# Weights of a fused attention and gated-FFN kernel: staged loads and casts replaced by casting DMAs, with the first batches reordered around them

## The chip, the cores and the metric

The kernel runs on one core of a Trainium2 chip. The metric is the device time of one execution in microseconds (us). A difference between the two kernels is told from medians of repeated runs on the same chip.

## The reference, cut to what matters

Eight batches of twelve heads, each 448 positions by 64 elements, go through an attention without softmax: squared ReLU of the scores, divided by the sequence length. The result, as 3584 tokens of 768 elements, goes through an RMS norm, a gated feed-forward layer of width 1536 and an output projection.

```python
scores = scale * np.matmul(q, k.transpose(0, 1, 3, 2))      # scale = 1/8
attn = np.maximum(scores, 0.0) ** 2 / S                     # S = 448
x = np.matmul(attn, v)            # to (batch*position, head*element) = (3584, 768)
xn = x / np.sqrt(np.mean(x * x, -1) + 1e-06) * rms_g
g, val = xn @ w_gate, xn @ w_val                            # 768 x 1536 each
out = (g / (1 + np.exp(-g)) * val) @ w_out                  # 1536 x 768
```

All inputs and the output are float32 in DRAM. The kernel computes in bfloat16 with sums in float32.

## The kernel before, in words

Work goes batch by batch. Everything of a batch is kept transposed: 128 partitions hold the elements of a pair of heads, 448 columns hold the positions. There are six such pairs (`KT` = `HP` = 6), and twelve blocks of 128 hidden columns (`FT` = 12).

**Attention.** `pe_transposes` (L158) brings one head pair of q and k to PSUM by TensorE, and a copy (L165 on ScalarE for batch 1, L167 on VectorE for batch 0) puts it in `qkT`. Scores of a quarter of the positions (`scores` L201, `pair_scores` L221) go to a two-bank PSUM tile of a pool of two (`ps_s`); ScalarE, or VectorE for one quarter in four, applies the ReLU (L211, L231, L229) and VectorE squares it (L270). `attend` (L287) multiplies with v, and `leave` writes the scaled x (`xT`, L303) and its square (`x`, L304). A step that does one quarter of one head pair is called a visit here. From batch 2 on the transposes of q and k are made by DMA (L177, L181), with fills on the Pool queue (L189, L190).

**Swap.** Each gate and value matmul uses 64 of the 128 rows of TensorE, so two run side by side, one on each half of the partitions. Twelve heads are needed on both halves, so `swap` (L312) copies the upper half of `xT` to the lower half of `xD` and the reverse, by two DMAs.

**Gate and value.** `rounds` (L442) makes one block: six rounds on `xT` (own rounds), then six on `xD` (swapped rounds), two matmuls a round. Its weights are one 128-column slice of `wgv_sb`. `block_second` ends with SiLU on ScalarE (L483) and a product on VectorE (L485).

**Norm.** `norm_stat` sums the squares by TensorE (L405), takes the root on ScalarE (L412) and the reciprocal on VectorE (L416). `norm_apply` multiplies six tiles of `xT` in place (L421) and swaps them again, three pairs to a swap. For batch 0 the gate and value sums of blocks 0 to 2 are taken early, from x that is not yet normalized; `early_out` copies them out of PSUM (L454) and `early_rest` multiplies them with the reciprocal later (L460, L464, L466).

**Loads.** q, k, v and the first two 256-column slices of gate and value weights (blocks 0 to 3) come through casting DMAs on the Pool queue (L95, L111). The weights of blocks 4 to 11 come as float32 through the SP queue into four staging buffers (`fetch_raw`, L130), and Pool casts them (`cast_raw`, L141). `fetch_o` (L118) loads the output weights in six casting DMAs, between the casts. The staging buffers hold the space that the `kT` pool takes once they are closed (`unstage`), so the DMA transposes of batch 2 come after them.

**Order of the work.** Each engine runs its instructions in the order in which the program writes them. `weave` writes a main list and puts side steps between its units by position. For batch 0 the main list is `gate_value(0, EB)`, blocks 3 to 11, and the visits of batch 1 are its side steps. Then `out_tiles(0, 0, 3)` makes three output tiles (L405, L500), with the norm of batch 1 behind the first half tile; then follow the blocks of batch 1 with the visits of batch 2, and so on to batch 7. The loads of batch 2 (`fetch(2)`) stand behind the weights on the Pool queue, then the fills of batch 2, then `fetch(3)`.

Of the kernel before, what the change touches and what calls it, by code (L numbers as in the profile page):

```python
# [34 lines left out]
def kernel(  # L35
# [11 lines left out]
    nc = tc.nc  # L47
# [72 lines left out]
    stage = {}  # L120

    def fetch_raw(which, s):

        st = late["stage"].tile([P, H, P], FP32, name="wst", tag="wst")
        if which == "o":
            dst = st[:].rearrange("p a b -> p (a b)").rearrange("p (a b) -> p a b", a=2)
            i = nc.sync.dma_start(out=dst, in_=wo_rows(moe_w_out, s))
        else:
            for prt, src in gv_slices(s * P, (s + 1) * P):
                i = nc.sync.dma_start(out=st[prt], in_=src)  # L130
        stage[which, s] = st
        return i

    def cast_raw(which, s):
        src = stage.pop((which, s))[:]
        if which == "o":
            src = src.rearrange("p a b -> p (a b)").rearrange("p (a b) -> p a b", a=2)
            dst = wo_sb[:, 2 * s : 2 * s + 2, :]
        else:
            dst = wgv_sb[:, :, s * P : (s + 1) * P]  # L140
        return nc.gpsimd.tensor_copy(out=dst, in_=src)  # L141

# [6 lines left out]
    swapped = []  # L149
    HH = H // 2  # L150

    def pe_transposes(b, j):
# [155 lines left out]
    def swap(b, j0, j1, eng=None):  # L308

        swapped.append(b)  # L310
# [6 lines left out]
    def attention_first(b):  # L317
# [22 lines left out]
        add(leave, (HP - 2,))  # L340
        add(attend, (HP - 1,))
        add(leave, (HP - 1,))
        add(swap, 3, HP, nc.scalar)
        return units

    def attention_second(b):

        steps = [lambda: pe_transposes(b, 0)]
# [12 lines left out]
        for j in range(HP):  # L361
            for c in range(NCH):
                steps.append(lambda j=j, c=c: visit(j, c))
                if c == 0 and j + 1 < HP:
                    steps.append(lambda j=j: pe_transposes(b, j + 1))
# [41 lines left out]
    def norm_stat(b):  # L407
        psSS = ps_m.tile([P, S], FP32, name="psSS", tag="mm")
# [10 lines left out]
    def norm_apply(b, k0=0, k1=KT, eng=None):  # L419
        for kt in range(k0, k1):  # L420
            i = nc.vector.tensor_tensor(  # L421
                out=xTs[b][:, kt, :], in0=xTs[b][:, kt, :], in1=rstds[b][:], op=ALU.mult
            )
            if kt % 3 == 2:
                swap(b, kt - 2, kt + 1, eng)
        return i
# [7 lines left out]
    def rounds(b, fb, parts, r0, r1):  # L434

        for r in range(r0, r1):
            kt, own = r % KT, r < KT
            src = (xTs if own else xDs)[b]
# [18 lines left out]
    def early_rest(b, fb):  # L457

        t = early.pop(fb)
        nc.vector.tensor_tensor(  # L460
            out=t[:], in0=t[:], in1=rstds[b][:].unsqueeze(1).to_broadcast([P, 2, S]), op=ALU.mult
        )
        s = spool.tile([P, S], BF16, name="sil", tag="sil")
# [97 lines left out]
    def hold(i, until, reason):  # L561

        i, until = (x.ins if hasattr(x, "ins") else x for x in (i, until))
        tc.add_manual_dep(
            i,
            until.name,
            mybir.DependencyInfo(mybir.DependencyClass.Sync, mybir.DependencyReason.DATA),
            reason=reason,
        )

# [3 lines left out]
    for h0 in (0, HH):  # L574
        load("q", 1, h0, h0 + HH)
        load("k", 1, h0, h0 + HH)
    load("v", 1)
    def trans_fill(b, half):
# [3 lines left out]
    raws = [("gv", s) for s in range(4, FT)]  # L582
    NST, EB = 4, 3
    with tc.tile_pool(name="qkT", bufs=2, side="right") as tp, tc.tile_pool(
        name="early", bufs=EB, side="right"
    ) as ep:
        stages = ExitStack()
        late["stage"] = stages.enter_context(tc.tile_pool(name="stage", bufs=NST))
        late["qkT"], late["early"] = tp, ep
        warm(12)  # L590
        for n, fn in enumerate(attention_first(0)):
# [3 lines left out]
            if swapped and "raw" not in late:  # L595
                late["raw"] = [fetch_raw(*w) for w in raws[:NST]]
        fed = [0]
        held = {}
# [104 lines left out]
```

## Time and profile before

| what | value |
|---|---|
| median of 3 runs | 485.09 us (483.44 to 486.19) |
| the profiled execution: its own time | 487.38 us |
| the profiled execution: span from first to last instruction | 485.6 us |
| mean granted TensorE clock | 0.966 |
| DRAM read, written | 47.19 MB, 11.01 MB |
| busy: PE, DVE, ACT, POOL | 94%, 55%, 58%, 12% of the span |

All views below are of that one execution, with times from the start of its span. PE is TensorE, DVE VectorE, ACT ScalarE, POOL GpSimd, SPq and ACTq the DMA issuing of SP and ACT. A row of the timeline gives start, duration, engine, line, operation, what is written and read, and how many instructions were merged; in brackets stands the idle time ahead of it and what ended that. KB of a DMA and the GB/s of a stretch count bytes as they are written, so a casting load of 384 KB reads 768 KB. PEclk is the clock that TensorE was granted, as a share of full speed.

### The profile page before, as it was taken

The page shows a single profiled execution, that of the slowest core. Times are in us where ns is not written, and L with a number is a line of the kernel's source. Part 1 is how long each engine was busy: PE and PEld are TensorE (multiplying, and loading weights), DVE is VectorE, ACT ScalarE, POOL GpSimd, SP SyncE. Part 2 cuts the span into 40 slices and gives each one's busy share as a digit, 9 for nine tenths or more (in the row PEclk, how much of TensorE's full clock was granted, in tenths as well). Part 3 has the DMA queues.
Part 4 walks back from the last instruction along what each step waited for, and adds up shares of the span by engine and source line. Part 5 has one row for each costly group of instructions (what it writes and reads, how often), then busy time and mean ns, then how long its engine had stood idle before and what let it go on. Part 6 is the DMA issues. An engine that isn't in the chain of part 4 may idle for free.

```text
span 485.6 us, 10871 instructions
## 1 busy us (share of the span) xinstructions
PE 454.9 (94%) x4744; PEld 252.1 (52%) x4744; DVE 268.8 (55%) x309; ACT 282.0 (58%) x417; POOL 60.2 (12%) x79
## 2 busy tenths in 40 slices
PE   7986488995999999999999999999999999999996
PEld 2333245462555655565555655555556655565664
DVE  2865556651677546647675556647664667552210
ACT  3782557761676667756675667665775467562221
POOL 7301432303000030000300030002100000000000
PEclk8897779998899999999999999999999999999999
DMA  9999998999940199606990399508990640023013
GB/s 106 196 214 197 202 214 142 131 172 195 205 86 1 34 210 193 96 2 125 189 165 22 90 190 188 64 21 181 173 124 2 149 125 1 1 62 95 1 34 99
DMA packets 92431, 57.03 MB, mean 117 GB/s; under 512 B 36576, under 2 KB 85728, under 8 KB 92384
## 3 DMA queue, kind: packets, MB, share of 16 engines
q0 software_dynamic: 38672, 24.58, 35.3%
q1 hardware_dynamic: 53232, 30.73, 33.1%
q10 hardware_dynamic: 480, 1.03, 1.0%
q8 instruction: 37, 0.61, 0.5%
q14 instruction: 10, 0.08, 0.0%
HBM read 47.19 MB, written 11.01 MB: 120 GB/s over the span
## 4 chain that ended last, share of the span: by engine, by line
PE 78%; DMA 7%; ACT 4%; DVE 4%; SPq 3%; issue 1%; POOL 0%; ACTq 0%; POOLq 0%
PE psG L442 32%; PE psO L405 19%; PE psV L442 10%; PE psAV L287 7%; PE psS L242 6%; DMA xD<-xT 4%; SPq L130 3%; DMA wst<-in_moe_w_gate_dram 2%; DVE xT L421 1%; DVE rstd L416 1%; PE psSS L405 1%; PE psS L201 1%; DMA kb<-in_k_dram 1%; PE psW L559 1%; PE psS L221 1%
## 5 line engine op out<-in xcount | busy, mean ns | idle before, releaser
L442 PEld LDWEIGHTS <-wgv_sb 64*128 64x128 bf16 x2304 | 124.5, 95 | 114.6 <-issue 30.7
L442 PE MATMUL psG<-xD,wgv_sb 64*128 64x448 bf16 x558 | 123.8, 353 | 4.0 <-DMA xD<-xT 4.0
L442 PE MATMUL psV<-xD,wgv_sb 64*128 64x448 bf16 x558 | 123.3, 354 | 4.1 <-DMA xD<-xT 4.0
L442 PE MATMUL psV<-xT,wgv_sb 64*128 64x448 bf16 x558 | 122.9, 354 | 0.0
L442 PE MATMUL psG<-xT,wgv_sb 64*128 64x448 bf16 x558 | 122.9, 354 | 0.0
L485 DVE TENSOR_TENSOR hT<-sil,psV 128x448 bf16<-128x448 bf16 x93 | 57.6, 619 | 113.9 <-ACT sil L483 113.0
L405 PE MATMUL psO<-wo_sb,hT 128*64 128x512 bf16 (+1 forms) x1344 | 113.7, 326 | 0.0
L256 ACT ACTIVATE r<-psS 112x896 bf16<-112x896 f32 x108 | 96.1, 917 | 25.3 <-PE psS L242 25.2
L405 PEld LDWEIGHTS <-hT 128*64 128x64 bf16 x1344 | 74.8, 110 | 36.2 <-issue 4.1
L483 ACT ACTIVATE sil<-psG 128x448 bf16<-128x448 f32 x93 | 50.6, 544 | 67.6 <-PE psV L442 36.9
L260 DVE TENSOR_TENSOR r<-r 112x1792 bf16<-112x1792 bf16 x72 | 78.4, 1089 | 12.8 <-ACT r L256 11.7
L500 ACT COPY ost<-psO 128x512 f32<-128x512 f32 (+1 forms) x56 | 26.7, 477 | 50.3 <-PE psO L405 43.4
L242 PE MATMUL psS<-qT,kT 64*128 64x448 bf16 (+1 forms) x288 | 49.2, 354 | 2.0 <-DMA qT<-qT 1.7
L416 DVE RECIPROCAL rstd<-rstd 128x448 f32<-128x448 f32 x8 | 23.6, 2953 | 43.2 <-ACT rstd L412 43.2
L287 PE MATMUL psAV<-r,vb 112*64 112x448 bf16 x384 | 41.7, 356 | 1.3 <-DVE r L270 1.3
L303 ACT ACTIVATE xT<-psAV,ga_sb 128x448 bf16<-128x448 f32 x48 | 28.1, 630 | 25.0 <-PE psAV L287 25.0
L254 DVE TENSOR_SCALAR r<-psS 112x896 bf16<-112x896 f32 x36 | 39.0, 1084 | 5.3 <-PE psS L242 5.3
L189 POOL DMA_DIRECT2D qT<-qT x12 | 6.5, 539 | 267.4 <-DMA qT<-qb 117.3
L287 PEld LDWEIGHTS <-vb 112*64 112x64 bf16 x384 | 19.6, 110 | 21.9 <-issue 10.0
L421 DVE TENSOR_TENSOR xT<-xT,rstd 128x448 bf16<-128x448 bf16 x48 | 26.5, 618 | 3.4 <-DMA xD<-xT 3.1
L242 PEld LDWEIGHTS <-kT 64*128 64x128 bf16 (+1 forms) x288 | 17.7, 97 | 19.5 <-issue 8.5
L270 DVE TENSOR_TENSOR r<-r 112x1792 bf16<-112x1792 bf16 x23 | 26.8, 1182 | 0.6 <-ACT r L231 0.3
(51 smaller groups left out, 255.6 us busy)
## 6 DMA issues: line engine op xcount, KB each, us to landing
xD<-xT SPq DMA_DIRECT2D x30, 168.0 KB, 2.8
vb<-in_v_dram POOLq DMA_DIRECT2D x7, 672.0 KB, 18.2
qb<-in_q_dram POOLq DMA_DIRECT2D x6, 672.0 KB, 12.2
kb<-in_k_dram POOLq DMA_DIRECT2D x6, 672.0 KB, 13.9
qT<-qT POOLq DMA_DIRECT2D x24, 168.0 KB, 4.4
wst<-in_moe_w_gate_dram SPq DMA_DIRECT2D x8, 384.0 KB, 12.6
wst<-in_moe_w_val_dram SPq DMA_DIRECT2D x8, 384.0 KB, 13.6
out_dram<-ost SPq DMA_DIRECT2D x8, 336.0 KB, 4.6
```

The costliest lines, as they stand in the source:

```text
L242: nc.tensor.matmul(out=psS[: end - o, hf, :S], lhsT=flat[prt, o:end], rhs=qT[prt, 1 - hf : 3 - hf, h % HH], start=True, stop=True,)
L254: nc.vector.tensor_relu(out=r[:, cp], in_=src)
L256: nc.scalar.activation(out=r[:, cp], in_=src, func=ACT.Relu)
L260: nc.vector.tensor_tensor(out=r[:], in0=r[:], in1=r[:], op=ALU.mult)
L287: nc.tensor.matmul(out=part[hh * D : (hh + 1) * D, :], lhsT=ld["v", b][:, 2 * j + hh, c * D : (c + 1) * D], rhs=rsq[b, 2 * j + hh, c], sta ...
L303: nc.scalar.mul(out=xTs[b][:, j, :], in_=psAV[:, i, :], mul=ga_sb[:, j : j + 1])
L405: nc.tensor.matmul(out=ps[prt, :w], lhsT=lhsT[:, prt], rhs=rhs, start=start, stop=stop)
L416: nc.vector.reciprocal(out=rstd[:], in_=rstd[:])
L421: i = nc.vector.tensor_tensor(out=xTs[b][:, kt, :], in0=xTs[b][:, kt, :], in1=rstds[b][:], op=ALU.mult)
L442: nc.tensor.matmul(out=parts[part][:, :S], lhsT=wgv_sb[prt, h, fb * P : (fb + 1) * P], rhs=src[prt, kt, :], start=(r == 0), stop=(r == 2 * ...
L483: nc.scalar.activation(out=s[:], in_=psG, func=ACT.Silu)
L485: nc.vector.tensor_tensor(out=hT[:, fb, o : o + S], in0=s[:], in1=psV, op=ALU.mult)
```

## The change

Four things change, all of them before the output tiles of batch 0.

First, the staging goes away: no `fetch_raw`, no `cast_raw`, no staging pool. All weights come by casting DMAs on the Pool queue, gate and value in 256-column slices, queued at the start among the loads of batch 1. The `kT` pool is made at once.

Second, batch 0's swap of raw x is made pair by pair on SP, each behind its `leave`, instead of three pairs on SP and three on ACT. The two norm swaps move from ACT to SP.

Third, the normalized x of batch 0 goes to a second pair of buffers, so `norm_apply(0)` no longer waits for the readers of raw x. The early blocks now take all twelve rounds from raw x, block after block.

Fourth, the first two TensorE transposes of batch 1 move into the tail of batch 0's attention (their copies go to VectorE), and four visits and one more transpose of batch 1 go between the early blocks. The sum of squares of batch 0 moves to the other PSUM pool. `early_rest` is split, with its scaling ahead in the main list.

```diff
-        if b:
+        if b and j > 1:
             nc.scalar.copy(out=t[:], in_=psT[:])
...
             add(scores, j, (0, 1), (3,))
             if j > 1:
                 add(leave, (j - 2,))
-                if j == 4:
-                    add(swap, 0, 3)
+                add(swap, j - 2, j - 1)
...
         add(leave, (HP - 2,))
+        add(swap, HP - 2, HP - 1)
         add(attend, (HP - 1,))
         add(leave, (HP - 1,))
-        add(swap, 3, HP, nc.scalar)
+        add(swap, 5, HP)
...
+        src = xTs[b]
+        if b == 0:
+            xTs[b] = npool.tile([P, KT, S], BF16, name="xT", tag="xT", bufs=2)
+            xDs[b] = npool.tile([P, KT, S], BF16, name="xD", tag="xD", bufs=2)
+        for kt in range(KT):
+            nc.vector.tensor_tensor(
+                out=xTs[b][:, kt, :], in0=src[:, kt, :], in1=rstds[b][:], op=ALU.mult
             )
             if kt % 3 == 2:
-                swap(b, kt - 2, kt + 1, eng)
-        return i
+                swap(b, kt - 2, kt + 1)
...
         load("k", 1, h0, h0 + HH)
+    for s in range(2, 4):
+        fetch_gv(s)
     load("v", 1)
+    for s in range(4, NSL):
+        fetch_gv(s)
+    for s in range(FT // 2):
+        fetch_o(s)
+    late["kT"] = pool("kT", 2)
...
+            if n == len(first) - 3:
+                pe_transposes(1, 0)
+            if n == len(first) - 1:
+                pe_transposes(1, 1)
             fn()
...
-        rounds(0, 0, blocks[0], 0, KT)
+        raw_x = xTs[0], xDs[0]
+        blocks = [early_block(0)]
+        rounds(0, 0, blocks[0], 0, KT, raw_x)
         norm_stat(0)
...
-        rounds(0, 0, blocks[0], KT, KT + 3)
-        for fb in range(1, EB):
-            rounds(0, fb, blocks[fb], 0, KT + 3)
-        for fb in range(EB):
-            rounds(0, fb, blocks[fb], KT + 3, 2 * KT)
-            early_out(0, fb, blocks[fb])
-        feed(2)
-        norm_apply(0, 0, 3, nc.scalar)
+        steps.pop(0)()
+        rounds(0, 0, blocks[0], KT, 2 * KT, raw_x)
+        early_out(0, 0, blocks[0])
+        norm_apply(0)
+        for fb in range(1, EB):
+            blocks.append(early_block(fb))
+            steps.pop(0)()
+            rounds(0, fb, blocks[fb], 0, KT, raw_x)
+            steps.pop(0)()
+            rounds(0, fb, blocks[fb], KT, 2 * KT, raw_x)
+            early_out(0, fb, blocks[fb])
         main = gate_value(0, EB)
...
-        sides += [(9, unstage), (9.1, lambda: fetch(2))]
+        sides += [(9.1, lambda: fetch(2))]
```

On the Pool queue before, from the load of batch 1's v on. `wst` is a staging buffer, `wgv_sb` the gate and value weights, `wo_sb` the output weights.

```order
L95 DMA vb<-in_v_dram 112x12x256
L141 CAST wgv_sb<-wst 128x12x128 x3
L118 DMA wo_sb<-in_moe_w_out_dram 128x2x768
L141 CAST wgv_sb<-wst 128x12x128
L118 DMA wo_sb<-in_moe_w_out_dram 128x2x768
```

The same queue now, from four weight loads ahead of that v to batch 2's q:

```order
L111 DMA wgv_sb<-in_moe_w_gate_dram 64x12x256
L111 DMA wgv_sb<-in_moe_w_val_dram 64x12x256
L111 DMA wgv_sb<-in_moe_w_gate_dram 64x12x256
L111 DMA wgv_sb<-in_moe_w_val_dram 64x12x256
L95 DMA vb<-in_v_dram 112x12x256
L111 DMA wgv_sb<-in_moe_w_gate_dram 64x12x256
L111 DMA wgv_sb<-in_moe_w_val_dram 64x12x256
L111 DMA wgv_sb<-in_moe_w_gate_dram 64x12x256
L111 DMA wgv_sb<-in_moe_w_val_dram 64x12x256
L118 DMA wo_sb<-in_moe_w_out_dram 128x2x768 x6
L95 DMA qb<-in_q_dram 112x12x256
```

Nothing computes on Pool here any more, and batch 2's loads stand directly behind the last weights.

On ScalarE before, from batch 0's last `leave` (L304 writes the squares) to the first SiLU of an early block. `rstd` is the root of the norm, `gv` the early sums, `psS` scores.

```order
L304 ACTIVATE x_264<-psAV 128x448
L312 DMA xD<-xT 64x1344 x2
L412 ACTIVATE rstd<-psSS,eps_col 128x448
L415 ACT_TABLE_LOAD
L415 ACTIVATE warm_act<-eps_col 128x1
L454 COPY gv<-psE 128x448 x6
L312 DMA xD<-xT 64x1344 x2
L165 COPY qkT<-psT 128x896
L312 DMA xD<-xT 64x1344 x2
L464 ACTIVATE sil<-gv 128x448
L231 ACTIVATE r<-psS 112x896
```

The same stretch of ScalarE now (L280 is L304, L390 is L412, L207 is L231, L436 is L454, L468 is the SiLU of block 3):

```order
L280 ACTIVATE x_278<-psAV 128x448
L390 ACTIVATE rstd<-psSS,eps_col 128x448
L393 ACT_TABLE_LOAD
L393 ACTIVATE warm_act<-eps_col 128x1
L207 ACTIVATE r<-psS 112x896
L436 COPY gv<-psE 128x448 x2
L207 ACTIVATE r<-psS 112x896 x2
L436 COPY gv<-psE 128x448 x2
L141 COPY qkT<-psT 128x896
L436 COPY gv<-psE 128x448 x2
L207 ACTIVATE r<-psS 112x896 x2
L468 ACTIVATE sil<-psG 128x448
```

ScalarE issues no DMA there any more, and takes three ReLUs and one copy of batch 1 between the early sums.

On the SP queue now, from the load of the norm's gains to batch 2's first transposes:

```order
L530 DMA g_sb<-in_moe_rms_g_dram 128x6x1
L287 DMA xD<-xT 64x448 x12
L287 DMA xD<-xT 64x1344 x4
L153 DMA_TRANSPOSE qT<-qb 128x12x112
L157 DMA_TRANSPOSE kT<-kb 128x12x112
```

Before, sixteen staging loads stood between the first swap and the first transpose of this queue; now only swaps do.

More of the change, by code (lines that the diff above doesn't have):

```diff
@@ L148 @@
     raw, psAVs = {}, {}
-    swapped = []
     HH = H // 2
@@ L462, in early_rest @@
         )
+    def early_rest(b, fb):
+        t = early.pop(fb)
         s = spool.tile([P, S], BF16, name="sil", tag="sil")
@@ L594 @@
                 warm(2)
[L595 to L598, printed above, removed]
-        def feed(n):
-            while fed[0] < min(n, len(raws)):
-                i = cast_raw(*raws[fed[0]])
-                if fed[0] in held:
-                    hold(i, held[fed[0]], "casts on Pool keep out of the first batch's norm")
-                if fed[0] + NST < len(raws):
-                    fetch_raw(*raws[fed[0] + NST])
-                fed[0] += 1
@@ L609, in unstage, with early_block @@
-        def unstage():
-            feed(len(raws))
-            stages.close()
-            late["kT"] = pool("kT", 2)
-        steps = attention_second(1)
-        blocks = []
-        for fb in range(2):
-            psS = ps_s.tile([P, 2, 512], FP32, name="psE", tag="psS")
-            blocks.append((psS[:, 0, :], psS[:, 1, :]))
-        rounds(0, 0, blocks[0], 0, KT)
+        def early_block(fb):
+            return [ps_m.tile([P, S], FP32, name="psE", tag="mm")[:] for _ in range(2)]
+        raw_x = xTs[0], xDs[0]
```

73 lines of the change are left out of this document (18 added, 55 removed).

## The prediction

> **What bounds the kernel now.** I read the page's slices first, then the busy time by stretch, then the timeline where TensorE is not full.
>
> ```profile
> PE   7986488995999999999999999999999999999996
> ```
>
> Forty slices of 12 us: TensorE is full from the eleventh on. Only the first ten can give anything back.
>
> ```profile
> 12.00:24.00 12.00, 11.64 (x104) 4.32 (x105) 10.52 (x12) 8.96 (x13) 4.01 (x5) 0.83 1.45 195
> ...
> 36.00:48.00 12.00, 8.12 (x69) 3.76 (x69) 6.34 (x7) 3.08 (x5) 1.60 (x2) 0.81 1.22 197
> ...
> 60.00:72.00 12.00, 9.56 (x81) 4.57 (x81) 6.24 (x7) 5.72 (x8) 3.98 (x4) 0.70 1.19 216
> ...
> 108.00:120.00 12.00, 6.88 (x75) 4.16 (x72) 3.10 (x6) 2.25 (x4) 4.29 (x6) 0.93 1.13 183
> 120.00:132.00 12.00, 12.00 (x99) 6.09 (x96) 6.46 (x8) 6.91 (x9) 0.00 (x0) 0.78 1.33 241
> ...
> 144.00:156.00 12.00, 12.00 (x128) 6.35 (x127) 8.69 (x11) 8.17 (x12) 0.00 (x0) 1.00 0.01 1
> ```
>
> Columns: stretch, length, then busy time of PE, PEld, DVE, ACT and POOL, granted clock, DMA share, GB/s. A full stretch holds 128 matmuls. Two holes stand out, in 36 to 72 us and in 108 to 132 us, each with a lower clock and busy DMA engines. The timeline of TensorE and ScalarE names the waits of the first:
>
> ```profile
> 34.64 1.31 PE L442 MATMUL psE<-xT,wgv_sb 64*128 64x448 bf16 x12
> 35.88 1.33 PE L405 MATMUL psSS<-x,ones_bf 128*64 128x448 bf16 x12
> 37.14 0.74 PE L442 MATMUL psE<-xD,wgv_sb 64*128 64x448 bf16 x6
> ...
> 43.74 0.53 PE L442 MATMUL psE<-xD,wgv_sb 64*128 64x448 bf16 x1 [2.45 <-DMA xD<-xT]
> 45.70 3.51 PE L442 MATMUL psE<-xD,wgv_sb 64*128 64x448 bf16 x17 [1.44 <-DMA xD<-xT]
> ...
> 51.86 2.43 ACTq L312 DMA_DIRECT2D xD<-xT  x2
> ...
> 55.77 0.37 PE L221 MATMUL psS<-qkT 64*128 64x448 bf16 x2 [2.01 <-ACT r L231]
> ...
> 58.88 0.53 PE L442 MATMUL psV<-xD,wgv_sb 64*128 64x448 bf16 x1 [1.88 <-DMA xD<-xT]
> ...
> 62.92 0.53 PE L442 MATMUL psV<-xD,wgv_sb 64*128 64x448 bf16 x1 [1.19 <-DMA xD<-xT]
> ...
> 63.62 0.58 PE L442 MATMUL psV<-xD,wgv_sb 64*128 64x448 bf16 x1
> ```
>
> TensorE waits for the swap of raw x (43.74, 45.70), then for that of normalized x (58.88 to 62.92). ScalarE, stuck 2.43 us issuing swaps, holds up a ReLU in between. And after the waits a matmul takes 0.53 to 0.58 us.
>
> **The first hole, step by step.** Before, the last matmul of block 3 starts at 63.62 and runs into the next; I count the block to 64.0.
>
> Work between 34.64 and there: six own rounds take 35.88 - 34.64 = 1.24, the sum of squares 37.14 - 35.88 = 1.26. By the full stretch a matmul costs 12.00 / 128 = 0.094 us, so a block of 24 costs 2.25, four cost 9.0. A visit has two matmuls, 0.2 us. A transpose step, from the chain of waits:
>
> ```profile
> 17.86 0.52 PE psT L158 x16
> ```
>
> Before, this span holds four blocks, the sum, three visits and two transposes: 9.0 + 1.3 + 0.6 + 1.0 = 11.9 of 64.0 - 34.6 = 29.4 us. So 17.5 us are waits and slow clock.
>
> Now it holds six visits and one transpose (the other, first of batch 1, hides in the wait ahead of the last `attend`; the second adds 0.5 ahead of block 0). That is 0.5 + 9.0 + 1.3 + 1.2 + 0.5 = 12.5, so 47.1 if nothing waited. Two swaps can make it wait. Their prices, from the DMA issues (last column: us from issue to landing), the first pair's own issue ahead:
>
> ```profile
> 27.29 1.19 SPq L312 DMA_DIRECT2D xD<-xT  x2
> ...
> xD<-xT SPq DMA_DIRECT2D x2, 168.0 KB, 5.8
> ...
> xD<-xT ACTq DMA_DIRECT2D x2, 168.0 KB, 9.5
> ...
> xD<-xT SPq DMA_DIRECT2D x30, 168.0 KB, 2.8
> ```
>
> The first pair met mostly the Pool queue's casting loads; the second, on ACT some 8 us later, also the staging loads on SP; 2.8 is the median over the whole kernel. After the change only the Pool queue runs beside them, so I take 5.8, with 2.8 and 9.5 as bounds. The timeline gives the steps around them:
>
> ```profile
> 34.27 0.63 ACT L303 ACTIVATE xT<-psAV,ga_sb 128x448 bf16<-128x448 f32 x1
> ...
> 37.25 0.63 ACT L412 ACTIVATE rstd<-psSS,eps_col 128x448 f32<-128x448 f32 x1 [1.91 <-PE psSS L405]
> ...
> 37.91 2.95 DVE L416 RECIPROCAL rstd<-rstd 128x448 f32<-128x448 f32 x1 [4.16 <-ACT rstd L412]
> ...
> 40.96 1.70 DVE L421 TENSOR_TENSOR xT<-xT,rstd 128x448 bf16<-128x448 bf16 x3
> ...
> 45.73 1.69 DVE L421 TENSOR_TENSOR xT<-xT,rstd 128x448 bf16<-128x448 bf16 x3 [3.08 <-DMA xD<-xT]
> ```
>
> Raw x: the last pair is written at 34.9, its second DMA goes out 0.6 later (1.19 for two) and lands at 41.3. TensorE gets to the last round of block 0 at 34.6 + 0.5 + 1.2 + 1.3 + 0.2 + 1.0 = 38.8 and waits 2.5 us. Blocks 1 and 2 then end near 46.9, or 49 at a slow clock. Normalized x: the sum of squares ends at 37.6, root at 38.3, reciprocal at 41.2, six products at 44.6, with no wait between the two threes now (3.08 before, the second buffer's worth). The last swap DMA goes out at 45.2 and lands at 51.0; the last rounds take 0.6. Block 3 ends at 51.6, as this chain and not block 0's wait sets it. Gain 64.0 - 51.6 = 12.4, and three visits and a transpose (1.1) are done ahead: **13.5 us**. At 2.8 it would be 16.4, at 9.5 it is 9.8.
>
> Does the slow clock go too? Before, 0.70 over 60 to 72 is half speed for 7.2 of 12 us, so to about 67; from 64 on that costs 1.5 us. The row at 45.70 shows 17 matmuls in 3.5 us, twice the usual time, after waits of only 2.45 and 1.44. [...] The row speaks against it, so I give the 1.5 us against jams of VectorE in blocks 4 to 11, which gets three scalings there, and count nothing.
>
> **Removed at nothing.** Eight casts on Pool and the staging loads were off TensorE's path except through the contention priced above. Two copies of transposed q and k come to VectorE ahead of the reciprocal, which waits 4.16 us for the root; without that cover they would delay it by about 1.1 (two tiles, at the 0.57 of a product).
>
> **Do the weights come in time?** All now queue on Pool, in order. Until 24 us nothing moves but this queue, at 195 GB/s in 12 to 24 (190 KB a us). Sizes and landings from the DMA issues, one issue and the first output tile from the timeline:
>
> ```profile
> wgv_sb<-in_moe_w_gate_dram POOLq DMA_DIRECT2D x2, 384.0 KB, 13.8
> ...
> wo_sb<-in_moe_w_out_dram POOLq DMA_DIRECT2D x6, 384.0 KB, 9.1
> ...
> qb<-in_q_dram POOLq DMA_DIRECT2D x6, 672.0 KB, 12.2
> ...
> 9.20 0.81 POOL L111 DMA_DIRECT2D wgv_sb<-in_moe_w_gate_dram  x1
> ...
> 99.38 2.78 PE L405 MATMUL psO<-wo_sb,hT 128*64 128x512 bf16 x24
> ```
>
> By 24 us (9.20 + 13.8, and the next two loads) the first 3552 KB are in: 2016 of batch 0, 4 x 384 of weights. Then at 190 KB a us: batch 1's q and k (1344) at 31, blocks 4 to 7 (1536) at 39, v (672) at 43, blocks 8 to 11 at 51, output weights (2304) at 63, batch 2 (2016) at 73; 12 x 56 + 4 x 168 KB of swaps add up to 7. TensorE needs block 4 at 52, block 8 four blocks of 2.25 later at the earliest, 61, output weights at 99.4 less 13.5, 86. There is room of 10 us and more everywhere. Tightest is batch 1's first q and k, needed at about 32 by the transpose moved forward, 2 to 3 us ahead of block 0; their first halves stand before all added loads and are due at 24 + 672 / 190 = 28.
>
> **The second hole.** The norm of batch 1, in the timeline and (last two rows) the DMA issues:
>
> ```profile
> 86.73 0.95 POOL L95 DMA_DIRECT2D qb<-in_q_dram  x1
> ...
> 109.57 4.44 SPq L312 DMA_DIRECT2D xD<-xT  x4
> ...
> 110.81 0.97 POOL L95 DMA_DIRECT2D qb<-in_q_dram  x1
> ...
> 115.53 0.35 PE L242 MATMUL psS<-qT,kT 64*128 64x448 bf16 x1 [1.69 <-DMA qT<-qT]
> ...
> 118.33 0.48 PE L442 MATMUL psG<-xD,wgv_sb 64*128 64x448 bf16 x1 [2.46 <-DMA xD<-xT]
> 119.78 0.53 PE L442 MATMUL psV<-xD,wgv_sb 64*128 64x448 bf16 x1 [0.97 <-DMA xD<-xT]
> ...
> xD<-xT SPq DMA_DIRECT2D x4, 168.0 KB, 8.4
> ...
> qb<-in_q_dram POOLq DMA_DIRECT2D x1, 672.0 KB, 9.6
> ```
>
> Here 1.69 + 2.46 + 0.97 = 5.1 us are waits, and the clock of 0.78 over 12 us costs 2.6: 7.7 us. Batch 2's fills and batch 3's q collide with the swap. Batch 2's q was issued at 86.73, batch 3's 24.1 us later. Now batch 2's q lands near 72 (63, then its own 672 KB and most of the swaps; before 86.7 + 9.6 = 96.3); keeping the 14.5 us from there to batch 3's q, that one goes out at 86 to 88, and its three loads take 2016 / 190 = 10.6 us, to 97 or 99. The swap comes at 109.5 - 13.5 = 96. So the fills are out of the way (1.7) but the tail of `fetch(3)` may still meet the swap: 5.8 in place of 8.4 saves up to 2.6 more. I take **4.5 us**; bounds are 0 and 7.7. After 132 us TensorE is full and nothing changes.
>
> **Sum.** 13.5 + 4.5 = 18.0. Against the profiled execution, 487.4 - 18.0 = 469.4. That execution lies 2.3 above the median of the runs; taken off the median, 485.1 - 18.0 = **467**.
>
> **Rivals.**
>
> *The swaps still take 9.5 us* under a Pool queue that is full to 80 us. For: the DMA engines are no less busy than before. Against: the 5.8 row. First hole 9.8, second 4.5: 485 - 14.3 = 471.
>
> *The second hole stays*, moved up with the rest, because `fetch(3)` meets the swap again. 485 - 13.5 = 471.5. For: the 86 to 99 window against 96. Against: the fills are done earlier.
>
> *Both holes close*: quiet swaps and the clock kept: 16.4 + 7.7 + 1.5 = 25.6, so 459.5. For: staging moved twice the bytes of the cast weights. Against: the Pool queue stays full past the first norm.
>
> *Slower: the single Pool queue starves.* [...] It decides when the output weights come after 99.4 + 4.5 = 104 us, where the gain is spent: 7392 KB after 24 us, so below 7392 / 80 = 92 KB a us, half of what 12 to 24 shows. At 80 KB a us they come at 116, and the time is near 485 + 12 = 497. The 12 to 24 row excludes most of it: VectorE busy for 10.52 of 12 us, and the queue at 195 GB/s, with issues of 0.81 us. [...]
>
> **How the numbers follow.** Forecast (462 to 468.5) 0.52; slow swaps 0.13; second hole stays 0.13; both close 0.12; the change gives little (the moved transposes wait for q and k, and jams eat the rest) 0.04; slower 0.06. About 0.5% (2.4 us) is what a measurement of this kernel can tell from no change. Faster 0.90, same 0.04, slower 0.06. The range of 8 in 10 takes in the rivals on the faster side with 2.5 us of jams on top of 471.5: 458.5 to 475.
>
> **What would show it.** Right: block 3 ending near 52, no wait above 3 us in 36 to 60, first output tile near 86, waits at batch 1's norm under 3 us. Wrong: TensorE waiting for `wgv_sb` or `wo_sb` loads; swap landings of 9 us; the last tile of batch 0's blocks later than 92; ScalarE or VectorE the releaser of most waits in 52 to 86.

## The result, and the profile after

The changed kernel takes 471.8 us (median of 4 runs, 471.3 to 474.0), the kernel before 485.1 beside it: ratio 0.974, 95% interval 0.970 to 0.978. A second set of runs gave 471.3 and 0.973 (0.970 to 0.977). The change is 13.3 us faster, the forecast was 18.

The profiled execution of after took 472.2 us, its span is 470.2. Its row of TensorE in forty slices:

```profile
PE   6997899979999999999999999999999999999995
```

The slices below 9 in 36 to 72 us have thinned to one 7 and one 8; one hole is left, in the ninth slice. The same stretches as before show both places, after:

```profile
36.00:48.00 12.00, 9.19 (x71) 4.42 (x68) 7.31 (x9) 6.24 (x10) 3.10 (x5) 0.86 1.46 205
48.00:60.00 12.00, 10.64 (x127) 5.58 (x125) 8.05 (x9) 8.74 (x15) 4.00 (x5) 1.00 1.29 210
60.00:72.00 12.00, 11.01 (x131) 6.20 (x128) 9.64 (x14) 9.12 (x14) 0.93 (x1) 1.00 1.26 205
72.00:84.00 12.00, 11.24 (x116) 6.58 (x113) 7.30 (x10) 8.61 (x13) 1.09 (x2) 1.00 1.41 184
...
96.00:108.00 12.00, 8.79 (x79) 4.50 (x77) 2.71 (x5) 3.26 (x5) 0.00 (x0) 0.90 1.16 244
108.00:120.00 12.00, 11.65 (x115) 6.48 (x113) 9.68 (x11) 8.29 (x12) 0.00 (x0) 0.96 0.02 6
```

From 48 us on the clock is full (1.00) until the second hole. The DMA engines move 184 to 210 GB/s up to 84 us, in 44 to 60 us most of it for the queue of casting loads (2.60 of 3.31 MB), so the swaps of the first norm still run beside it. The timeline of TensorE through the first hole, up to the first output tile:

```profile
35.47 1.42 PE L424 MATMUL psE<-xT,wgv_sb 64*128 64x448 bf16 x12
...
40.60 0.35 PE L424 MATMUL psE<-xD,wgv_sb 64*128 64x448 bf16 x1 [1.41 <-DMA xD<-xT]
41.74 0.35 PE L424 MATMUL psE<-xD,wgv_sb 64*128 64x448 bf16 x1 [0.79 <-DMA xD<-xT]
42.36 0.35 PE L424 MATMUL psE<-xD,wgv_sb 64*128 64x448 bf16 x1 [0.27 <-DMA xD<-xT]
43.04 0.35 PE L424 MATMUL psE<-xD,wgv_sb 64*128 64x448 bf16 x1 [0.33 <-DMA xD<-xT]
...
45.01 2.71 PE L424 MATMUL psE<-xD,wgv_sb 64*128 64x448 bf16 x12
...
49.48 1.31 PE L424 MATMUL psE<-xD,wgv_sb 64*128 64x448 bf16 x12
...
53.91 0.35 PE L424 MATMUL psV<-xD,wgv_sb 64*128 64x448 bf16 x1 [0.70 <-DMA xD<-xT]
...
86.43 2.76 PE L380 MATMUL psO<-wo_sb,hT 128*64 128x512 bf16 x24
```

The waits for the swap of raw x add to 2.8 us, twelve matmuls then take 2.71 (1.31 one block later, at full speed), and block 3 waits 0.70 for the swap of normalized x. It ends near 54.5, before at 64.0. The first output tile starts at 86.43, before at 99.38.

The norm of batch 1 in the timeline of after, with the issues of its swap (SPq) and of batch 3's loads:

```profile
86.68 0.99 POOL L95 DMA_DIRECT2D qb<-in_q_dram  x1
91.24 0.96 POOL L95 DMA_DIRECT2D kb<-in_k_dram  x1 [3.58 <-issue]
92.19 0.94 POOL L95 DMA_DIRECT2D vb<-in_v_dram  x1
...
96.54 2.68 SPq L287 DMA_DIRECT2D xD<-xT  x4
...
103.15 0.35 PE L424 MATMUL psG<-xD,wgv_sb 64*128 64x448 bf16 x1 [2.29 <-DMA xD<-xT]
104.12 0.35 PE L424 MATMUL psV<-xD,wgv_sb 64*128 64x448 bf16 x1 [0.62 <-DMA xD<-xT]
105.49 0.51 PE L424 MATMUL psV<-xD,wgv_sb 64*128 64x448 bf16 x1 [0.23 <-DMA xD<-xT]
```

The DMA issues of after in 86 to 95 us, the loads of batch 3 (last column: us from issue to landing):

```profile
qb<-in_q_dram POOLq DMA_DIRECT2D x1, 672.0 KB, 9.2
kb<-in_k_dram POOLq DMA_DIRECT2D x1, 672.0 KB, 8.0
vb<-in_v_dram POOLq DMA_DIRECT2D x1, 672.0 KB, 16.0
```

The k and v of batch 3 land at 99.2 and 108.2 (issue plus landing), and the swap issued at 96.54 lies among them. Its landing stands in the DMA issues of 94 to 104 us:

```profile
xD<-xT SPq DMA_DIRECT2D x4, 168.0 KB, 6.8
```

Cutting each profiled execution in three makes all runs comparable: up to the first matmul on x (start), from there to the first output matmul (middle), and from there to the end of the span (rest). Before is 34.6 + 64.7 + 386.2, after is 35.5 + 51.0 + 383.8. So of the 15.4 us between the two spans 13.8 lie in the middle, 2.4 in the rest, and 0.8 is given back by a later start.

### The profile page after: what moved, and what is told of

Its sections match the earlier page's. It is cut to its first block, busy times and chain, and to the rows that moved or that the text cites. A ratio compares the mean times of both kernels' runs of the same rounds, so it can differ in the third digit from the quotient of the medians.

```text
span 470.2 us, 10856 instructions
## 1 busy us (share of the span) xinstructions
PE 450.9 (96%) x4748; PEld 252.0 (54%) x4748; DVE 265.8 (57%) x311; ACT 280.0 (60%) x415; POOL 53.6 (11%) x79
## 3 DMA queue, kind: packets, MB, share of 16 engines
HBM read 47.19 MB, written 11.01 MB: 124 GB/s over the span
## 4 chain that ended last, share of the span: by engine, by line
PE 83%; DVE 5%; DMA 5%; ACT 4%; issue 1%; POOL 1%; SPq 0%; POOLq 0%
PE psG L424 32%; PE psO L380 20%; PE psV L424 10%; PE psAV L263 9%; PE psS L218 6%; DMA xD<-xT 4%; DVE xT L404 2%; DVE rstd L394 2%; PE psSS L380 1%; PE psW L544 1%; PE psS L177 1%; DMA kb<-in_k_dram 1%; PE psT L134 1%; ACT r L207 1%; ACT r L187 1%
## 5 line engine op out<-in xcount | busy, mean ns | idle before, releaser
L424 PE MATMUL psG<-xD,wgv_sb 64*128 64x448 bf16 x558 | 121.9, 350 | 2.4 <-DMA xD<-xT 2.3
L424 PE MATMUL psV<-xD,wgv_sb 64*128 64x448 bf16 x558 | 121.6, 350 | 1.8 <-DMA xD<-xT 1.8
L424 PE MATMUL psV<-xT,wgv_sb 64*128 64x448 bf16 x558 | 121.6, 351 | 0.0
L468 ACT ACTIVATE sil<-psG 128x448 bf16<-128x448 f32 x93 | 50.7, 545 | 65.3 <-PE psV L424 36.9
L236 DVE TENSOR_TENSOR r<-r 112x1792 bf16<-112x1792 bf16 x72 | 78.4, 1090 | 12.7 <-ACT r L232 11.7
L485 ACT COPY ost<-psO 128x512 f32<-128x512 f32 (+1 forms) x56 | 26.8, 478 | 50.2 <-PE psO L380 44.0
L246 DVE TENSOR_TENSOR r<-r 112x1792 bf16<-112x1792 bf16 x23 | 24.5, 1086 | 0.1
## 6 DMA issues: line engine op xcount, KB each, us to landing
qb<-in_q_dram POOLq DMA_DIRECT2D x6, 672.0 KB, 12.4
```

What stands on the lines that cost most here:

```text
L236: nc.vector.tensor_tensor(out=r[:], in0=r[:], in1=r[:], op=ALU.mult)
L424: nc.tensor.matmul(out=parts[part][:, :S], lhsT=wgv_sb[prt, h, fb * P : (fb + 1) * P], rhs=src[prt, kt, :], start=(r == 0), stop=(r == 2 * ...
L468: nc.scalar.activation(out=s[:], in_=psG, func=ACT.Silu)
```

## The experiments

The three parts come from each kernel's profiled execution, the median from its runs. The kernels were timed in three groups of four, each group on one chip (the second and third on the same one) and beside the kernel before (484.6 us in the first, 485.9 in the second, 485.2 in the third), so ratios are given too.

| kernel | start | middle | rest | median | ratio to before, interval |
|---|---|---|---|---|---|
| before | 34.6 | 64.7 | 386.2 | 485.1 | |
| after | 35.5 | 51.0 | 383.8 | 471.8 | 0.974 (0.970 to 0.978) |
| after_again | 35.2 | 50.2 | 383.6 | 471.3 | 0.973 (0.970 to 0.977) |
| cast_only | 32.9 | 56.8 | 383.6 | 472.8 | 0.976 (0.972 to 0.981) |
| norm_in_place | 35.8 | 60.5 | 377.9 | 474.9 | 0.980 (0.976 to 0.984) |
| hold_fetch3 | 36.0 | 53.1 | 378.2 | 466.4 | 0.962 (0.958 to 0.966) |
| cast_hold | 35.1 | 55.1 | 377.9 | 470.5 | 0.968 (0.963 to 0.974) |
| batch2_first | 35.5 | 50.8 | 386.1 | 473.7 | 0.976 (0.972 to 0.979) |
| weights_wait | 36.7 | 50.4 | 384.2 | 471.6 | 0.972 (0.967 to 0.976) |
| visits_in_main | 34.2 | 55.3 | 382.2 | 471.9 | 0.973 (0.969 to 0.977) |
| hold_again | 36.9 | 50.4 | 377.8 | 465.8 | 0.959 (0.956 to 0.963) |
| cast_hold_again | 34.9 | 55.8 | 377.5 | 470.0 | 0.969 (0.966 to 0.972) |
| visits_hold | 36.8 | 55.6 | 377.6 | 471.0 | 0.970 (0.967 to 0.973) |
| before_hold | 35.2 | 63.5 | 378.3 | 479.0 | 0.985 (0.981 to 0.990) |

The start, 32.9 to 36.9, varies between executions of kernels that are alike up to there, and so does the middle: hold_fetch3 and hold_again are one kernel, with 53.1 and 50.4. A difference of under 3 us between two single values of that column proves nothing. The rest takes two kinds of values: 377.5 to 378.3 in the seven executions without a wait for the second norm's swap of over 0.5 us, 382.2 to 386.2 where the hole is there. So the hole costs 4 to 8.5 us, 6 of them in after and 8 in before.

Two theories stood at first. **Queue theory**: the gain is that the staged float32 loads no longer run beside the swaps, and what waits are left come from loads queued beside a swap. **Order theory**: the second buffer and the visits between the early blocks make the gain, and the leftover waits are set by the norm's chain of products.

**The change again**, for the spread of runs:

> The changed kernel itself, as the yardstick on this chip. Every theory: within 0.5% of 471.8 us; TensorE waits for the swap of raw x (about 2.8 us) and for that of normalized x (0.7 us) in the first hole, and 3.1 us for the swap of batch 1's norm.

471.3 us: the same.

**Only the loads** (cast_only). Before, with its staging taken out and the loads of the change put in; order, swaps and products in place as before:

```diff
     load("k", 1, h0, h0 + HH)
+for s in range(2, 4):
+    fetch_gv(s)
 load("v", 1)
+for s in range(4, NSL):
+    fetch_gv(s)
+for s in range(FT // 2):
+    fetch_o(s)
+late["kT"] = pool("kT", 2)
...
-        feed(2)
...
-        sides += [(9, unstage), (9.1, lambda: fetch(2))]
+        sides += [(9.1, lambda: fetch(2))]
```

> The kernel before with the weights loaded as the change does it, and nothing else of the change: old order, old swaps, norm in place. Queue theory (the gain comes mostly from taking the staged loads off the DMA engines): most of the gain, 474 to 478 us, swaps on ACT landing in 6 to 8 us instead of 9. Order theory (the gain comes from the second buffer and the visits between the early blocks; the loads only make room for it): 480 to 485 us, the wait of 3.1 us for the norm's second three products still there, and the second hole smaller by 2 to 3 us.

472.8 us, beyond what either theory gave: 1.5 from the changed kernel on the same chip, with intervals that overlap. Its timeline: the products on VectorE, then TensorE at the normalized swap and at the first output matmul:

```profile
39.19 3.30 DVE L421 TENSOR_TENSOR xT<-xT,rstd 128x448 bf16<-128x448 bf16 x6
...
49.93 0.35 PE L442 MATMUL psG<-xD,wgv_sb 64*128 64x448 bf16 x1 [2.55 <-DMA xD<-xT]
51.83 0.53 PE L442 MATMUL psV<-xD,wgv_sb 64*128 64x448 bf16 x1 [1.55 <-DMA xD<-xT]
53.66 0.53 PE L442 MATMUL psV<-xD,wgv_sb 64*128 64x448 bf16 x1 [0.33 <-DMA xD<-xT]
...
89.65 2.57 PE L405 MATMUL psO<-wo_sb,hT 128*64 128x512 bf16 x22
```

The wait of 3.08 us before the second three products, which the order theory expected to stay, is gone, though the products are still written in place: the last wait for the second half of raw x's swap ended 7.4 us after ScalarE began to issue it (33.16 to 40.55), before 10.8 (34.93 to 45.70). The normalized swap itself landed no faster (8.9 us, 8.1 and 9.2 before), but ScalarE issued it from 42.5 us on, from 49.3 before. Block 3 ends at 54.7, about as early as in after, but the first matmul on x of this execution also came 2.6 us earlier. Counted from the first matmul on x, block 3 ends after 29.4 us in before, 21.8 in cast_only (20.7 and 20.3 in the two later kernels with these loads and a hold) and 19.0 in after. So the loads alone give most of the gain up to there, without second buffer and without visits ahead. This run takes away the staging loads and the casts on Pool together, and batch 2 comes earlier with them; it doesn't tell these apart. Its main list is longer, 35.0 us from the end of block 3 to the first output matmul against 31.9 in after. The profiled execution was this kernel's longest (475.4).

**Products in place** (norm_in_place). After, with batch 0's products in `xT` and so behind the last reader of raw x:

```diff
     def norm_apply(b):
         src = xTs[b]
-        if b == 0:
-            xTs[b] = npool.tile([P, KT, S], BF16, name="xT", tag="xT", bufs=2)
-            xDs[b] = npool.tile([P, KT, S], BF16, name="xD", tag="xD", bufs=2)
...
         early_out(0, 0, blocks[0])
-        norm_apply(0)
         for fb in range(1, EB):
...
             early_out(0, fb, blocks[fb])
+        norm_apply(0)
```

> The changed kernel with batch 0's products written in place, so after the early blocks' last matmul on raw x instead of beside them. If the chain root, reciprocal, products, swap sets the end of block 3: the products start about 50 instead of 41.8 us, block 3 ends near 62 instead of 54.5, and the time is 5 to 8 us more (477 to 480). If TensorE has enough other work around block 3: under 2 us more (471 to 474).

474.9 us, 3.6 over after_again. In its timeline the wait for the swap is back, and the first output matmul comes ten us later:

```profile
58.80 0.53 PE L421 MATMUL psG<-xD,wgv_sb 64*128 64x448 bf16 x1 [4.87 <-DMA xD<-xT]
...
96.25 2.76 PE L380 MATMUL psO<-wo_sb,hT 128*64 128x512 bf16 x24
...
106.32 2.83 SPq L287 DMA_DIRECT2D xD<-xT  x4
```

The middle is 60.5, so in the new order the buffer is worth some 10 us there. But 5.7 come back in the rest: the second norm's swap is issued only at 106.32, after the last of batch 3's loads has landed (v, issued at 96.73, in 7.3 us); it lands in 2.8, and TensorE doesn't wait for it. Neither theory had seen that the two holes trade.

**Batch 3's loads behind the swap** (hold_fetch3). After, with a dependency:

```diff
-    fetch(3)
     weave(out_tiles(0, 0, full), [(1, lambda: norm_stat(1)), (1, lambda: norm_apply(1))])
+    hold(fetch(3)[0], applied[1], "third batch's loads keep out of the second norm's swap")
```

Here `applied[1]` is the last DMA of the swap, and the Pool queue sends batch 3's q only when that has landed.

> The changed kernel with batch 3's loads held back until the swap of batch 1's norm has landed. Queue theory: that swap lands in about 3 us instead of 6.8, the second hole's 4.9 us (3.1 of waits, 1.7 of slow clock) shrink to under 1, time 466 to 468 us. Rival, the hole is set by the norm chain and by TensorE running out of output tiles: the swap lands as late, time 471 to 473 us.

466.4 us, and no wait for the swap at the second norm: it landed in 2.6 us, where it took 6.7 in after_again. This and its repeat below are the fastest of all kernels here. That the second hole is batch 3's loads beside the swap is shown by taking away that one thing.

**Batch 2 ahead of the output weights** (batch2_first):

```diff
-    for s in range(FT // 2):
-        fetch_o(s)
...
+        fetch(2)
+        for s in range(FT // 2):
+            fetch_o(s)
...
-        sides += [(9.1, lambda: fetch(2))]
```

> The changed kernel with batch 2's three loads put ahead of the output weights on the Pool queue; nothing is held. In the changed kernel batch 2's q is issued at 56.9, lands at 74.0, and with it the transposes, the shifted copies and then batch 3's loads come late: those are issued from 86.7 on and land until 108, beside the second norm's swap (issued 96.5, landed 103). Queue theory: with batch 2 some 8 to 10 us earlier, batch 3's loads are issued near 77 to 80 and have landed before the second norm's swap is issued; the waits for xD of 3.1 us after 100 us and the half-speed matmuls behind them go, 467 to 469. The output weights then come later, near 72 to 76, still ahead of the first output tile at 86. Rival: batch 3's loads are set by the end of batch 0's and 1's use of their buffers and not by batch 2's landing; they stay at 86 to 92, the second hole stays, 471 to 472.5.

473.7 us: slower than either expected. Batch 2's q did land 12.5 us earlier (61.5 against 74.0), but its transposes then ran beside the output weights. The SP queue of this kernel:

```profile
61.59 3.43 SPq L153 DMA_TRANSPOSE qT<-qb  x1
65.29 12.13 SPq L157 DMA_TRANSPOSE kT<-kb  x1
77.48 7.68 SPq L153 DMA_TRANSPOSE qT<-qb  x1
85.21 6.58 SPq L157 DMA_TRANSPOSE kT<-kb  x1
```

In after these four begin at 74.0 and are all issued by 85.2. Here the last is issued by 91.8, so the fills behind them on the Pool queue go out at 96.5 and batch 3's three loads at 97.6 to 99.5, all at once on top of the swap issued at 96.4. TensorE waits longer than in after:

```profile
102.75 0.35 PE L424 MATMUL psV<-xD,wgv_sb 64*128 64x448 bf16 x1 [1.87 <-DMA xD<-xT]
107.05 0.53 PE L424 MATMUL psG<-xD,wgv_sb 64*128 64x448 bf16 x1 [3.58 <-DMA xD<-xT]
107.77 0.53 PE L424 MATMUL psV<-xD,wgv_sb 64*128 64x448 bf16 x1 [0.19 <-DMA xD<-xT]
```

More of batch 3 beside the swap, a longer wait: 5.6 us against 3.1, a rest of 386.1 against 383.8. The queue theory's cause stands; the date at which it thought the loads would come was wrong.

**Later weights behind the first swap** (weights_wait):

```diff
-    for s in range(4, NSL):
-        fetch_gv(s)
-    for s in range(FT // 2):
-        fetch_o(s)
...
+        for s in range(4, NSL):
+            fetch_gv(s, applied[0] if s == 4 else None)
+        for s in range(FT // 2):
+            fetch_o(s)
```

> The changed kernel with the weights of blocks 8 to 11, the output weights and so batch 2 behind them held on the Pool queue until the first norm's swap has landed. It measures what the loads that run beside that swap cost. Queue theory: the swap, which lands 7.8 us after its issue beside the casting loads, lands in 3 to 4 us; block 3 ends near 50.5 instead of 54.5 and the first output tile comes 3 us earlier, 468 to 469.5, if batch 2, some 5 us later than now, doesn't widen the second hole (issue of batch 3's loads at 91 to 96, all of them then beside the second swap; it costs back 0 to 3). [...]

471.6 us, no change. The swap did land early, by the DMA issues of 44 to 60 us:

```profile
xD<-xT SPq DMA_DIRECT2D x4, 168.0 KB, 2.6
```

In after it is 7.8 in the same place. Block 3 no longer waits at all, and yet its middle is that of after_again (50.4 and 50.2). The early blocks in its timeline tell why:

```profile
41.70 0.35 PE L429 MATMUL psE<-xD,wgv_sb 64*128 64x448 bf16 x1 [1.31 <-DMA xD<-xT]
...
44.05 2.79 PE L429 MATMUL psE<-xT,wgv_sb 64*128 64x448 bf16 x12
...
46.67 2.75 PE L429 MATMUL psE<-xD,wgv_sb 64*128 64x448 bf16 x12
```

The swap of raw x, issued before the hold does anything, still makes TensorE wait, and the half-speed matmuls behind that fill the time up to 49 (clock 0.77 over 36 to 48 us, 0.86 in after). In after the two chains, the norm's with its swap and TensorE's own through the early blocks, end within 0.7 us of each other (the wait at 53.91); by that, taking one away gains no more than 0.7. No run takes both away. Here the queue theory failed in the time: behind the held loads the swap did land early, in 2.6 us, and the time stayed as it was.

**The visits back in the main list** (visits_in_main). The early blocks without steps of batch 1 between them:

```diff
-        steps.pop(0)()
         rounds(0, 0, blocks[0], KT, 2 * KT, raw_x)
...
-            steps.pop(0)()
             rounds(0, fb, blocks[fb], 0, KT, raw_x)
-            steps.pop(0)()
```

The two lines in the loop run twice, so these are five steps, four visits and a transpose (the text on record counts one visit too few).

> The changed kernel with the four steps of batch 1 that it runs between the early blocks (three visits and a transpose) back in the main list; products in the second buffer and everything else as in the change. Theory that the visits cover the waits for the products and their swap: without them each early block comes earlier and waits longer for the swap, block 3 no earlier, and the main list has 4 steps (some 2.5 us) more to do, +1.5 to +2.5: 473 to 474.3. Rival, after the run cast_only: steps of batch 1 cost the same in either place, the early blocks come earlier by as much, and the matrix unit's order around the wait is worth nothing, within 0.8 of the changed kernel: 471 to 472.5.

471.9 us: by the median the rival was right, and the visits are worth nothing. By the parts they are worth 4.4 in the middle (55.3 against 51.0), with 1.6 back in the rest, where the hole is smaller, and 1.3 from an earlier start of that execution. This and norm_in_place led to a third theory, the **sink theory**: with the hole open, time gained ahead of it comes partly back as a longer wait in it, because batch 3's loads drain at their own date.

**Loads with the hold** (cast_hold): cast_only with the edit of hold_fetch3.

> This is the kernel of the run cast_only (before with all weights as casting loads and nothing else of the change: old order of the early blocks, products in place, old grouping of the swaps), with batch 3's loads held until the second norm's swap has landed. Loads theory: the reordering and the second buffer are worth the 1 us between cast_only (472.8) and the changed kernel (471.3 to 471.8) and no more; with the second hole closed in both, this kernel comes to 466.5 to 468.5, at most 2 above the run hold_fetch3 (466.4), with no wait for xD after 84 us. Order theory: the reordering pulls the first output tile forward by 3 us (89.65 in cast_only, 86.43 in the changed kernel) and the second hole hid that; with the hole closed the 3 us come out, and this kernel stays at 469 to 471.

470.5 us. It speaks for the order theory's number, but the runs of the two kernels met (467.2 to 471.4 against 465.0 to 469.3, on different chips), so the last four kernels ran together, with more rounds.

> The kernel of the run hold_fetch3 (466.4) a second time, beside the next three on one chip, since runs of one kernel differ by 1 to 2 us. Both theories: 465.5 to 468.

> The kernel of the run cast_hold (470.5: before with weights as casting loads and batch 3's loads held, nothing else of the change) beside hold_again. Sink theory, formed after eight runs: the second norm's swap cannot land before batch 3's loads have drained, near 103 to 107 us in every kernel whose first output tile starts between 86 and 90, so what the reordering and the second buffer gain before that is eaten by a longer wait there; with the hole closed it shows, and this kernel is 2.5 to 4.5 us over hold_again. Loads theory: the difference between the two earlier runs (4.1 us, 467.2 to 471.4 against 465.0 to 469.3) was chance; at most 1.5 us over hold_again.

> The changed kernel with the four steps of batch 1 moved out of the early blocks to the main list (the run visits_in_main: 471.9, no slower than the changed kernel, though its first output tile starts at 89.5 instead of 86.4) and with batch 3's loads held until the second norm's swap has landed. Sink theory: the 3 us that the visits are worth at the first output tile come out once the second hole is closed: 2 to 3.5 over hold_again, 468.5 to 470. Rival: the steps cost the same in either place and the later output tile is made up elsewhere: within 1 of hold_again.

> The kernel before with one edit: batch 3's loads held until the second norm's swap has landed. It tests the forecast's reading of the second hole, where before waits 1.69 us for a shifted copy and 2.46 and 0.97 for the swap (115 to 120 us) with half-speed matmuls behind them, 7.7 in all. Queue theory: those waits are the swap and the copies lying behind batch 3's q on the DMA engines (issued 110.8, the swap 109.6); they go, and the half-speed stretch with them, 478 to 480.5. Rival: the swap is late by itself, since its products are; 483.5 to 486.

hold_again 465.8, cast_hold_again 470.0, visits_hold 471.0, before_hold 479.0. In the first, the Pool queue waits for the swap, and the DMA issues of 94 to 104 us give the swap's landing:

```profile
103.10 0.97 POOL L94 DMA_DIRECT2D qb<-in_q_dram  x1 [17.23 <-DMA xD<-xT]
```

```profile
xD<-xT SPq DMA_DIRECT2D x4, 168.0 KB, 2.8
```

With the hole closed, the ratios of hold_again (0.959, 0.956 to 0.963) and cast_hold_again (0.969, 0.966 to 0.972) lie apart: the reordering and the second buffer are worth 4.2 us, as the sink theory said, where with the hole open 1.5 was left of them. By medians the hold itself takes 6.2 off before and 4.9 off after, but only some 2.5 off cast_only and 1 off visits_in_main (cast_only against a kernel on another chip, visits_in_main against one of another group), while the rest of each profile shortens by 4.6 to 7.9. The profiled executions of cast_only and visits_in_main, whose rest is compared there, were the longest of their kernels; how large the hole is in a typical run of these two stays open. The visits are worth 5.2, more than the 2 to 3.5 expected. The stretch of visits_hold and one wait in its timeline show what they cost in the main list:

```profile
60.00:72.00 12.00, 9.48 (x116) 5.09 (x117) 11.02 (x15) 8.91 (x13) 1.88 (x2) 1.00 1.26 205
```

```profile
66.51 0.36 PE L196 MATMUL psS<-qkT 64*128 64x448 bf16 x2 [1.94 <-DVE r L204]
...
92.39 2.78 PE L380 MATMUL psO<-wo_sb,hT 128*64 128x512 bf16 x24
```

TensorE is busy for 9.48 of 12 us there, 11.01 in after: it waits for the ReLUs and squares of batch 1 on VectorE and ScalarE. A visit in the main list costs its share of those; between the early blocks it lies in time that TensorE waits for swaps anyway. And before_hold bears out the forecast's reading of the second hole of before: one dependency takes 6.2 us off the median of the kernel before, and its profile has no wait for that swap above 0.48 us. But only four of its six runs show the gain, 476.6 to 479.1 us; the other two took 485.2 and 485.9, as long as before, at mean clocks of 0.973 and 0.972, where the other four had 0.971 to 0.981. No profile shows those two, so why stays open.

From before to hold_again the steps add up, on one chip: the hold 6.2 (485.2 to 479.0), the casting loads 9.0 (to 470.0), reordering and second buffer 4.2 (to 465.8). The 6.2 and the 9.0 rest on the median 479.0 of all six runs of before_hold; by its four shorter runs they are 6.4 and 8.8. The change as made has the last two steps, and a smaller second hole.

## Why the prediction was right, and where it was off

It said 467 (458.5 to 475); 471.8 was measured. Its sum of 18.0 missed by 4.7, of which 2.1 come from the second hole, 0.5 from the first output tile and 1.9 from the base; the last 0.2 is between spans and times.

**First output tile: right in sum, wrong in its parts.** Forecast 13.5 earlier, to 86; it came 12.95 earlier, at 86.43. Block 3's end was to come 12.4 earlier and came 9.5 earlier. The step that failed is the swap's landing, taken as 5.8: the median of its four DMAs is 7.8, and the last of them, issued at 45.7 where 45.2 was forecast, took 8.2, to 53.9, where TensorE's wait ends. These 0.5 and 2.4 us are the whole miss (51.6 against 54.5). But the landing alone did not set the end, as weights_wait shows: the count of work, 47.1 if nothing waited, left out about 2 us (single matmuls between waits, own rounds of 1.34 where 1.24 was taken) and the half-speed block, so that TensorE's own chain came out nearly as late. The three visits and a transpose done ahead were priced at TensorE's time, 1.1; the main list after block 3 took 31.9 us in place of 35.4, a gain of 3.5. That the two misses nearly cancel in the sum is luck. The mis-sized term there is, at least in part, what a visit costs ScalarE and VectorE (five steps cost 4.4 us of the middle in visits_in_main); the slow clock behind block 3 is gone as well, and how the 3.5 divide is not shown. One sign that the forecast named for being wrong did come: between 54.5 us and the first output tile every wait of TensorE above 0.2 us is released by ScalarE or VectorE, 2.4 us in five waits. Before has 2.8 us of such waits behind block 3, so they took nothing from the gain.

**The slow clock.** The forecast counted nothing for it, on the ground of the row with 17 matmuls in 3.51 us after waits of 2.45 and 1.44. Half speed did come behind short waits: after has it behind waits of which the longest is 1.41 us (twelve matmuls in 2.71, clock 0.57 over 44 to 48 us). But that stretch lies ahead of block 3's end; behind it the clock is 1.00 up to 96 us, so the 1.5 us that the forecast set against jams were gained. The rows of after show half speed after 2.8 us of waits in pieces within 4 us. The sum of such waits doesn't decide it alone: in after_again the clock falls to 0.86 over 36 to 48 us after 2.1 us of them, in hold_again it stays at 1.00 over the same stretch after 2.3. What decides it is not shown.

**Weights in time: right.** TensorE waits for no weight in after. No run shows the 80 KB a us of the rival that starves the Pool queue: over 12 to 24 us of after the DMA engines moved 196 GB/s, with VectorE busy for 10.16 of 12. Batch 2's q was due near 72 to 73; it landed 17.1 us after its issue at 56.89, at 74.0.

**Second hole: mechanism right, size wrong.** Forecast 4.5 of 7.7; measured in the rest 2.4 of 8. The date of batch 3's q was right (86 to 88; it went out at 86.68), though by errors that cancel, since batch 2's q landed 2 us later and batch 3's followed 12.7 us behind it, not 14.5; right, too, was that its tail would meet the swap. The step that failed is "its three loads take 2016 / 190 = 10.6 us, to 97 or 99": k and v went out 4.6 and 5.5 us after q, and v landed at 108.2. For 3.58 us of that gap the profile names no releaser, so its cause stays open. The swap in front of that tail landed in 6.8, not 5.8, and the half-speed matmuls behind the waits cost 1.7 (clock 0.90 and 0.96 over 12 us each); the waits add to 3.1, where under 3 was a sign of being right. The same swap on the same SP queue landed in 2.8 us where Pool held its loads (hold_again) and in 6.8 where it didn't (after). The rival "second hole stays", 471.5, was the nearest to the result.

**The base.** The profiled execution of before lies 2.3 above its median, that of after 0.4. A gain worked out on the first (15.2 between the two profiled executions) was taken off the median, which moved by 13.3.

**The reason given.** The forecast gave the first hole to two things, quieter swaps and products that no longer wait for readers of raw x. The runs give most of it to the loads: with products in place they end block 3 7.6 to 9.1 us earlier than before, where after gains 10.4 (counted from the first matmul on x). The 3.08 us that the forecast called the second buffer's worth go with the loads alone, in cast_only. In the change the second buffer is needed because the new order puts the blocks' readers of raw x, with visits between them, behind the products; its own worth and the visits' come out fully only when the second hole is closed.

## What to carry to other kernels

When a gain at one place shows only in part, cut the executions at a point between the two places and compare the pieces: here the piece after the first output tile took two values 4 to 8.5 us apart, and that named the next thing to mend. A prefetch that can go out 16 us later at no cost (batch 3's q at 103.1 in hold_again, at 86.7 in after) should wait for the small copy that is needed at once: beside the prefetch that copy took 6.8 us to land, ahead of it 2.8, and one dependency was worth 4.9 us on after, and 6.2 on before in four runs of six. Price a step that is moved by every engine it uses, and by how busy that engine is at the place it leaves.

## What the runs showed of the hardware that was not expected

The landing of a swap depended little on its size beside the casting loads, with 206 and 207 GB/s moved in the two stretches that follow. The DMA issues of after in 24 to 34 us, for one pair of heads, and in 44 to 60 us, for three:

```profile
xD<-xT SPq DMA_DIRECT2D x6, 56.0 KB, 5.6
```

```profile
xD<-xT SPq DMA_DIRECT2D x4, 168.0 KB, 7.8
```

A third of the bytes landed in 5.6 in place of 7.8, while the 168 KB landed in 2.6 to 3.3 where no load lay beside them (2.6 in weights_wait, 2.8 in hold_again, 3.3 for two of its four DMAs in before_hold). The first swap of three pairs before landed in 5.8, so a single pair took as long to land as three. The landings of the DMA transposes differed more. The DMA issues of batch2_first in 62 to 76 us, and of after in 74 to 86 us:

```profile
qT<-qb SPq DMA_TRANSPOSE x1, 16.9
kT<-kb SPq DMA_TRANSPOSE x1, 24.3
```

```profile
qT<-qb SPq DMA_TRANSPOSE x2, 6.0
kT<-kb SPq DMA_TRANSPOSE x2, 6.5
```

In the first stretch the Pool queue, with the output weights, moved 2.26 MB in 14 us, in the second, with the rest of batch 2 and its first fills, 1.06 MB in 12 us. Beside the fuller queue a transpose took about three to four times as long to land. That is what turned an earlier batch 2 into a later batch 3.
